# A fused recurrent attention and feed-forward kernel: half of unit 0's r and k in the gate's memory, its stateless products first, and TensorE's early waits filled with zeros

## The chip, the cores and the metric

The kernel runs on one core of one Trainium2 chip. The metric is the device time of one execution in microseconds (us). One more execution is recorded by the hardware profiler; its span runs from the first to the last instruction.

## What is computed

For 4 batches, 8 heads, 768 tokens and heads of 48, a recurrence with a state of 48 x 48 per head runs over the tokens, and its output goes through a feed-forward layer from 384 to 2048 and back, all in float32:

```
for t in range(S):
    kt, vt, rt, wt = (k[:, :, t], v[:, :, t], r[:, :, t], w[:, :, t])
    cur = np.einsum('bhd,bhe->bhde', u[None] * kt, vt)
    y[:, :, t] = np.einsum('bhd,bhde->bhe', rt, state + cur)
    state = wt[:, :, :, None] * state + np.einsum('bhd,bhe->bhde', kt, vt)
x = y.transpose(0, 2, 1, 3).reshape(B * S, H * D)
h = x @ w_in
g = np.where(h >= 1, h, np.where(h <= -1, 0.0, (h + 1) ** 2 / 4.0))
out = g @ w_out
```

## The kernel before, in words

**Units.** The 3072 tokens of all batches are cut into 12 units of 256 tokens; three units make a batch, and units 0, 3, 6 and 9 start from an empty state. In a unit the heads are split into two halves q of 128 rows, and the tokens into chunks of 64. `attention(u, ...)` lays out one unit:

- Loads on SyncE's queue: per half the scales w (`wq`, 128 x 521) and r and k together (`rk`, 128 x 1024); then v. For `wq` and `rk` there are three slots each, `slot = [(2u + 1 - q) % 3 ...]`: unit 0 takes slots 0 and 1, unit 1 takes 2 and 0. So unit 1's second load of r and k goes where unit 0's first half lies.
- VectorE scans: p, the running product of the scales (L473), and y, its inverse from the chunk's end (L468), one half after the other. Then k times y (L494) and r times p (L544), in place.
- For units 0 to 2, ScalarE makes k times u (L484), and TensorE multiplies it with r (`among`, L514, 32 small matmuls, which the trace records as 64). The result gives the diagonal, which VectorE picks into the tiles R (L520). A second `among` of k and r gives what lies below the diagonal, and two more picks. ScalarE copies the transposed k (L553, `ktrans`) to SBUF (L560).
- `umat` (L575) makes each chunk's k'v. The states follow one another: VectorE adds the old state to it (L593) and multiplies by p at the chunk's end (L594). For unit 0 (`CHAINED`) TensorE adds instead (L598), and VectorE only multiplies (L591).
- The output `y`: products with the earlier states in two orders (`cross`, `along`, L620), and products of R with v (also L620). The last are stateless: they need no state. Units 0 and 1 (`ALONE`) begin with banks cleared by TensorE (L655) and add to them, then spread the last heads' rows with a permutation (L703), and subtract their high part with a matmul (L694, the "subtracting triples"), so that ScalarE can copy a high and a low part to x (L684, L680).

**Steps.** The 12 units make 6 blocks of 512 tokens. A step is one block (or half block) and one of 16 slices f of the hidden layer: nine matmuls into a bank h (L989), the gate on ScalarE and VectorE (L790, L791, L792, L794, L795, into buffers g, gh, gl, three each), and nine matmuls into the output banks acc two to three steps later (L1009). Block 0 does its first 5 slices half by half, block 1 its first 14. The outputs of a block are copied to ob and to two of the g buffers and leave from there (L822, L823).

**Weights.** A slice's bits are loaded (L390), split by ScalarE (L402, L404), given their sign by GpSimd (L406; for f 9 by VectorE, `SIGNS`), joined by VectorE (L408), rounded by ScalarE to the high part (L398; VectorE for the slices in `SPLITS`), and the low part is left by VectorE (L411). `FLIGHT` is how many may be under way.

**Checks.** ScalarE checks every unit's scales (L746, L747). For the first `GUARDED` units that is done late, on a second load of the scales into the buffers fl; for the others in place.

**Order.** `Plan` collects all operations with costs, dependencies and due times (`SLACK`, `LEADS`, `DECODE` set them), simulates the engines and a load queue and keeps the best order of some tries. The engines then run their lists in that order; a list waits where its next instruction waits. `kept_warm` walks TensorE's list and, where the plan expects a wait, puts in matmuls of zeros (L360) into a bank that is to be begun afresh, up to a share `USE` of the last 3.4 us. At the very start 50 small matmuls of zeros are issued (L366).

Of the kernel before, what the change touches and what calls it, by code (L numbers as in the profile page):

```python
# [10 lines left out]
F32 = mybir.dt.float32  # L11
# [15 lines left out]
C = 64  # L27
# [17 lines left out]
USE, SPAN, COLUMN = 0.68, 3.4, 0.00168  # L45

COLD = 7.0

# [8 lines left out]
class Plan:  # L57
# [97 lines left out]
    def kept_warm(self, order, engine, banks, fill):  # L155

        ops, begin, end = self.ops, self.begin, self.end
        free, out, busy = 0.0, [], []
        used = {b: [n for n in order if b in ops[n]["touch"]] for b in banks}
        for n in order:  # L160
            op = ops[n]
            if op["e"] == engine:
                at = begin[n]
                use = sum(max(0.0, y - max(x, at - SPAN)) for x, y in busy)
                lack = min(USE * SPAN - use, at - free - 0.3)
                if free and lack > 0.15:
                    for b in banks:
                        after = next((m for m in used[b] if begin[m] >= at), None)
                        before = max((end[m] for m in used[b] if begin[m] < at), default=0.0)
                        if (after is None or ops[after]["fresh"]) and at - max(before, free) > lack:  # L170
                            out.append(lambda b=b, lack=lack, free=free: fill(b, lack, free))
                            busy.append((at - lack, at))
                            break
                free = at + op["cost"]
                busy.append((at, free))
            out.append(op["emit"])
        return out

    def order(self):
# [24 lines left out]
        while any(open_.values()):  # L204
# [18 lines left out]
            begin[n] = t  # L223
            free[e] = end[n] = t + op["cost"]
            if op["port"]:
                port = end[n]
                first.clear()
            if op["size"]:
                bus = max(bus, t) + op["size"] / 360e3
                end[n] = bus + 2.0  # L230
                lands.append(end[n])
# [24 lines left out]

SLACK = 2.03
LEADS = {0: 71.6, 1: 72.9, 2: 33.1, 3: 10.6, 4: 28.8, 5: 10.1, 6: 29.8, 7: 24.3, 8: 36.5, 9: 16.8, 10: 13.8, 11: -2.7}
LEAD, DECODE = 15, 12.7
FLIGHT = 3  # L260
FULL = 3

EARLY = 3

GUARDED = 6

APART = 1

# [3 lines left out]

SPLITS = set()
SIGNS = {9}
CHAINED = {0}
STEP, FIRST, PACED = 4.9, 24.0, 4.6
# [3 lines left out]
def attention_moe(tc, a):  # L280
# [41 lines left out]
    last = one([128, 2, UT], F32R, "last")  # L322
    g_ = tiles(LAG + 1, [128, WIDE], F32, "g")
    gh = tiles(LAG + 1, [128, WIDE], F32R, "gh")
# [29 lines left out]

    def zeros(to, n):

        while n >= 32:
            m = min(512, n if n < 128 else n // 128 * 128)
            rhs = zero[:, 0:m] if m <= 128 else zero.unsqueeze(1).broadcast_to([128, m // 128, 128])
            PE.matmul(to[:, 0:m], lhsT=zero, rhs=rhs, start=True, stop=True)  # L360
            n -= m
# [64 lines left out]
    def attention(u, when):  # L426
# [15 lines left out]

        slot = [(2 * u + 1 - q) % 3 for q in range(2)]
        pv = p_.rearrange("p (q n) c -> p q n c", q=2)

# [3 lines left out]
        for q in (1, 0):  # L449
            load(due, wq[slot[q]], a["w"][u, q], [("w", slot[q])])  # L450
            load(due, rk[slot[q]], a["rk"][u, q], [("k", slot[q]), ("r", slot[q])])
        if u == 0:
# [25 lines left out]
        def parts(q, i):  # L478
            return rk[slot[q]][:, i].rearrange("p (n c) -> p n c", c=C)

        def with_u(q):
            for pr in range(2):
                cs = slice(pr * UT, pr * UT + UT)
                A.mul(ku[:, q, cs], rk[slot[q]][:, 1, cs], u_col[:, 2 * q + pr : 2 * q + pr + 1])  # L484

        for q in (1, 0):
            s = slot[q]
            if early:
                op("ACT", 1.0, due, [("k", s), "cst"], [("ku", q), "nk"], lambda q=q: with_u(q))
# [4 lines left out]
            op("DVE", 0.69, due, ["y"], [("k", s)], lambda q=q: V.tensor_tensor(  # L494
                out=parts(q, 1), in0=parts(q, 1), in1=y_.rearrange("p (n c) -> p n c", c=C + 1)[:, :, 1:], op=ALU.mult), port=True)
# [8 lines left out]
        def among(to, left):  # L504

            for pair in range(4):
                q, pr = divmod(pair, 2)
                for c2 in range(2):
                    for g in range(2):
                        for h in range(2):  # L510
# [4 lines left out]
                                bank[to[h]][HP * g : HP * g + C, lo : lo + C], lhsT=left(q)[i, cs],  # L515
                                rhs=rk[slot[q]][i, 0, cs], start=True, stop=True,
                            )
# [5 lines left out]

        both = [("r", slot[0]), ("r", slot[1])]
        if early:
# [17 lines left out]
        for q in (1, 0):  # L543
            op("DVE", 0.69, due, [("p", q)], [("r", slot[q])], lambda q=q: V.tensor_tensor(  # L544
                out=parts(q, 0), in0=parts(q, 0), in1=pv[:, q, :, 0:C], op=ALU.mult), port=True)
# [3 lines left out]
        def ktrans(q, b):  # L549
            for pr in range(2):  # L550
                for c2 in range(2):
                    lo = (pr * 2 + c2) * 128
                    PE.transpose(out=bank[b][:, lo : lo + 128], in_=rk[slot[q]][:, 1, tokens(q, 1, pr, c2)], identity=ident)  # L553

        op("PE", 1.2, due, [("k", slot[0]), ("k", slot[1]), *both], [("b", ba[0]), ("b", ba[1])],
           lambda: among(ba, lambda q: rk[slot[q]][:, 1]))
        for q in (1, 0):
            b = take()
            op("PE", 0.4, due, [("k", slot[q]), "cst"], [("b", b)], lambda q=q, b=b: ktrans(q, b))
            op("ACT", 0.6, due, [("b", b)], [("kt", q)], lambda q=q, b=b: A.copy(  # L560
# [61 lines left out]
        def inter(g, h, pair, c2):  # L622
            s = before[2 * c2 + g]
            if s is None:
# [3 lines left out]
            put(g, pair, h, c2, lhsT=st[s][i, pair * D : pair * D + M],  # L628
                rhs=rk[slot[q]][i, 0, tokens(q, 0, pr, c2, g)])

# [11 lines left out]
        def along():  # L642
            crossed(0)
            for two in (0, 2):
                for c2 in range(2):
# [13 lines left out]
        if alone:  # L659
            op("PE", 0.5, due, ["zero"], [("b", by[0]), ("b", by[1])], cleared)  # L660
        op("PE", 0.6, due, ss + [vk, ("r", slot[0]), ("r", slot[1])], [("b", by[0]), ("b", by[1])], cross, fresh=not alone)

        for g in range(2):
            op("ACT", 0.2, due, [("b", by[g])], [("look", g)], lambda g=g: A.copy(look[0:1, g : g + 1], bank[by[g]][0:1, 0:1]))
        op("PE", 1.65, due, ss + [("R", 0), ("R", 1), vk, ("r", slot[0]), ("r", slot[1])],
           [("b", by[0]), ("b", by[1])], along, fresh=False)

# [201 lines left out]
    with tc.manual_schedule(engines=None):  # L869
        for emit in plan.kept_warm(plan.best(step_ops, dues), "PE", [("b", i) for i in range(8)],  # L870
                                   lambda b, us, at: zeros(bank[b[1]], int(us / COLUMN / (2 if at < COLD else 1)))):
            emit()
# [204 lines left out]
```

## Time and profile before

| | |
|---|---|
| median of 3 runs | 521.43 us (520.64 to 522.26) |
| profiled execution | 520.55 us, span 519.0 us |
| mean granted TensorE clock | 0.998 |
| TensorE busy | 504.5 us, 97% |
| VectorE busy | 340.9 us, 66% |
| ScalarE busy | 299.2 us, 58% |
| GpSimd busy | 86.8 us, 17% |
| first products of the first step (L989) | begin at 32.43 us |

In the rows below a time is counted from the start of the span. A row of the timeline has start, length, engine, line, operation, output and inputs, the number of instructions, and in brackets the idle time ahead and what ended it. A row of a group has its count, busy time, mean in ns, and the idle time before with its releasers. A row of the waits says who waited for whom, the total, how often, and the longest. Engine names are PE (TensorE), DVE (VectorE), ACT (ScalarE), POOL (GpSimd), SPq (SyncE's queue).

### The profile page before, as it was taken

How to read it: one execution, taken by the hardware profiler on the slowest of the kernel's cores; microseconds unless marked ns; L12 is line 12 of the kernel's file. 1: busy time of each engine (PE TensorE's matmuls, PEld its weight loads, DVE VectorE, ACT ScalarE, POOL GpSimd, SP SyncE). 2: the span in 40 equal slices, each digit the busy share in tenths (PEclk: the TensorE clock that was granted, in tenths of full speed). 3: DMA queues.
4: the chain of work that ended last, by engine and by line, in shares of the span. 5: the costliest groups of instructions: out<-in, count | busy, mean ns of one | idle time of the engine just before them, and what ended most of it. 6: DMA issues, size and time to landing. Idle time of an engine off the chain costs nothing.

```text
span 519.0 us, 13075 instructions
## 1 busy us (share of the span) xinstructions
PE 504.5 (97%) x5550; PEld 419.4 (81%) x5550; DVE 340.9 (66%) x597; ACT 299.2 (58%) x615; POOL 86.8 (17%) x60
## 2 busy tenths in 40 slices
PE   7989999999999999999999999999999999999995
PEld 5768988887899998877778878788888787788884
DVE  5999999979797979543979535895353445233332
ACT  3688888878865566543646544565444435444441
POOL 1654627511303030101020101110000100000000
PEclk9999999999999999999999999999999999999999
DMA  8794916147714152302262203230100100100001
GB/s 309 292 366 168 354 63 230 51 138 230 245 44 157 55 205 52 117 2 77 74 208 52 114 0 124 88 128 1 63 1 0 42 18 12 67 1 0 1 0 66
DMA packets 21762, 54.69 MB, mean 105 GB/s; under 512 B 3008, under 2 KB 8640, under 8 KB 21696
## 3 DMA queue, kind: packets, MB, share of 16 engines
q1 hardware_dynamic: 21552, 53.65, 29.8%
q8 instruction: 45, 0.74, 0.6%
q14 instruction: 21, 0.17, 0.1%
q10 hardware_dynamic: 144, 0.13, 0.1%
HBM read 47.09 MB, written 4.72 MB: 100 GB/s over the span
## 4 chain that ended last, share of the span: by engine, by line
PE 80%; DVE 5%; DMA 5%; ACT 4%; issue 2%; POOL 1%; SPq 0%; POOLq 0%; DVEq 0%; ACTq 0%
PE acc L1009 34%; PE h L989 34%; PE bank L620 4%; PE bank L514 2%; DMA rk<-in_rk 2%; PE bank L575 2%; PE bank L553 2%; DMA wraw<-in_wbits 1%; DVE r L520 1%; DMA out_y<-g 1%; DVE p L473 1%; DMA fl<-in_w 1%; POOL wraw L406 1%; DVE wt L411 1%; DVE fl L408 1%
## 5 line engine op out<-in xcount | busy, mean ns | idle before, releaser
L989 PE MATMUL h<-x,wt 128*128 128x512 f32 (+1 forms) x1035 | 223.3, 362 | 1.2 <-DVE g L792 1.2
L989 PEld LDWEIGHTS h<-x,wt 128*128 128x128 f32 x1035 | 171.1, 188 | 32.6 <-DVE g L792 1.9
L1009 PE MATMUL acc<-gh,wt 128*128 128x512 f32 (+1 forms) x690 | 157.1, 362 | 0.0
L792 DVE SCALAR_TENSOR_TENSOR g<-g,h 128x512 f32<-128x512 f32 (+1 forms) x115 | 68.0, 593 | 103.3 <-ACT g L791 98.8
L1009 PEld LDWEIGHTS acc<-gh,wt 128*128 128x128 f32 x690 | 115.6, 188 | 21.2
L790 ACT ACTIVATE g<-h 128x512 f32<-128x512 f32 (+1 forms) x115 | 60.4, 525 | 117.4 <-PE h L989 112.5
L795 DVE TENSOR_TENSOR gl<-g,gh 128x512 fp32r<-128x512 f32 (+1 forms) x115 | 73.7, 642 | 32.1 <-ACT gh L794 31.5
L794 ACT CAST gh<-g 128x512 fp32r<-128x512 f32 (+1 forms) x115 | 62.6, 546 | 44.2 <-DVE g L792 42.6
L1009 PE MATMUL acc<-gl,wt 128*128 128x512 f32 (+1 forms) x345 | 86.9, 358 | 0.0
L1009 PEld LDWEIGHTS acc<-gl,wt 128*128 128x128 f32 x345 | 59.6, 188 | 10.9 <-DVE gl L795 0.2
L791 ACT ACTIVATE g<-g 128x512 f32<-128x512 f32 (+1 forms) x115 | 64.6, 562 | 3.2
L406 POOL TENSOR_SCALAR wraw<-fl 128x768 uint16<-128x768 f32 x15 | 48.8, 3279 | 46.4 <-ACT wraw L404 42.3
L540 POOL TENSOR_TENSOR r<-cst,d 128x512 f32<-128x512 f32 x18 | 18.8, 1065 | 195.8 <-PE bank L620 178.7
L473 DVE TENSOR_TENSOR_SCAN p<-wq,seeds 128x520 f32<-128x520 f32 x24 | 31.3, 1304 | 3.0 <-DMA wq<-in_w 2.2
L532 POOL TENSOR_TENSOR nk<-nk 128x768 f32<-128x768 f32 x9 | 17.0, 1885 | 84.5 <-DMA nk<-in_nk 84.5
L468 DVE TENSOR_TENSOR_SCAN y<-wq,seeds 128x520 f32<-128x520 f32 x24 | 30.5, 1270 | 0.8
L494 DVE TENSOR_TENSOR rk<-rk,y 128x512 f32<-128x512 f32 x24 | 18.0, 751 | 1.2 <-ACT nk L484 0.8
L620 PEld LDWEIGHTS bank<-rk,st 64*64 64x64 f32 (+1 forms) x656 | 12.2, 133 | 7.2 <-issue 3.6
L593 DVE TENSOR_TENSOR sm<-bank,st 128x192 f32<-128x192 f32 x37 | 13.1, 355 | 6.7 <-PE bank L575 5.7
L404 ACT ACTIVATE wraw<-wraw 128x768 uint16<-128x768 uint32 x16 | 17.3, 1084 | 0.2
L560 ACT COPY kt<-bank 128x512 f32<-128x512 f32 x24 | 13.6, 587 | 6.5 <-PE bank L553 5.5
L553 PE MATMUL bank<-cst,rk 128*128 128x128 f32 x96 | 14.9, 287 | 2.5 <-DVE rk L494 2.0
(102 smaller groups left out, 399.9 us busy)
## 6 DMA issues: line engine op xcount, KB each, us to landing
rk<-in_rk SPq DMA_DIRECT2D x24, 512.0 KB, 5.4
wraw<-in_wbits SPq DMA_DIRECT2D x16, 768.0 KB, 7.9
nk<-in_nk SPq DMA_DIRECT2D x9, 768.0 KB, 4.5
wq<-in_w SPq DMA_DIRECT2D x24, 260.5 KB, 2.8
vn<-in_v SPq DMA_DIRECT2D x12, 384.0 KB, 6.3
fl<-in_w SPq DMA_DIRECT2D x12, 260.0 KB, 4.2
out_y<-g SPq DMA_DIRECT2D x11, 256.0 KB, 2.4
x<-last SPq DMA_DIRECT2D x60, 32.0 KB, 2.3
```

What stands on the lines that cost most here:

```text
L406: op(on, 0.62 if f in SIGNS else 3.2, due, [("fl", k)], [("raw", f)], lambda: e.tensor_scalar(out=half(1), in0=s, scalar1=0.0, scalar2=327 ...
L468: V.tensor_tensor_scan(out=y_[:, ::-1], data0=w[:, SEG:0:-1], data1=sv[:, ::-1], initial=0.0, op0=ALU.mult, op1=ALU.add)
L473: V.tensor_tensor_scan(out=pv[:, q].rearrange("p n c -> p (n c)"), data0=w[:, 0:SEG], data1=sv, initial=0.0, op0=ALU.mult, op1=ALU.add,)
L553: PE.transpose(out=bank[b][:, lo : lo + 128], in_=rk[slot[q]][:, 1, tokens(q, 1, pr, c2)], identity=ident)
L620: PE.matmul(out=bank[by[g]][HP * half : HP * half + M, lo : lo + C], start=first, stop=False, skip_group_check=True, **kw)
L790: op("ACT", c, due, [("b", 6 + hk)], [("g", gk)], lambda: nc.scalar.activation(gs, hs, AF.Relu, scale=0.5, bias=0.5))
L791: op("ACT", c, due, (), [("g", gk)], lambda: nc.scalar.activation(gs, gs, AF.Square))
L792: op("DVE", 0.13 + 0.53 * k, due, [("b", 6 + hk)], [("g", gk)], lambda: nc.vector.scalar_tensor_tensor(out=gs, in0=gs, scalar=1.0, in1=hs, ...
L794: op("ACT", c, due, [("g", gk)], [("gh", gk)], lambda: nc.scalar.copy(ghs, gs))
L795: op("DVE", 0.15 + 0.5 * k, due, [("g", gk), ("gh", gk)], [("gl", gk)], lambda: nc.vector.tensor_tensor(out=gls, in0=gs, in1=ghs.bitcast(F ...
L989: nc.tensor.matmul(hp, lhsT=wx[f][:, cs], rhs=xt[:, j, :], start=n == 0, stop=n == 8)
L1009: nc.tensor.matmul(o[j], lhsT=wx[f][:, cs], rhs=gt, start=first and i == 0, stop=stop and i == 2, skip_group_check=True)
```

## The change

1. Unit 0's half 1 takes its r and k not in an `rk` slot but in the first two of the three g buffers, which become parts of one tile (`gates`). Slot 0 is thus free for unit 1 from the start.
2. In units 0 and 1 the stateless products (`inner`) come first, then the products with the states (`along`, `cross`); each was one list before, with the stateless ones last.
3. `kept_warm` fills planned waits of TensorE up to 16 us of its plan wholly, and up to 0.3 us beyond; and it may now add zeros to a bank that is already begun (`held`, without `start`), if TensorE itself wrote to it before and after.
4. The plan counts TensorE's operations before 9 us twice, and loads at 300 KB/us up to 8 us, 390 after.
5. The table of numbers that sets the order is new. `FLIGHT` goes from 3 to 8, `GUARDED` from 6 to 3, the slices 1, 4, 5, 8, 9 are rounded on VectorE, the signs of 9, 10, 14, 15 are made on VectorE, and no unit is `CHAINED`.

```diff
-                lack = min(USE * SPAN - use, at - free - 0.3)
+                lack = at - free - 0.3 if at > EAGER else at - free + LATE if at - free > 0.15 else 0.0
+                if at > EAGER:
+                    lack = min(USE * SPAN - use, lack)
...
+                        held = after is not None and before is not None and not ops[after]["fresh"] and all(
+                            ops[m]["e"] == engine for m in (before, after)) and end[before] <= free
...
-FLIGHT = 3
+FLIGHT = 8
...
-GUARDED = 6
+GUARDED = 3
...
-SPLITS = set()
-SIGNS = {9}
-CHAINED = {0}
+SPLITS = {1, 4, 5, 8, 9}
+SIGNS = {9, 10, 14, 15}
+CHAINED = set()
...
+        rks = [rk[s] for s in slot]
+        rkey, kkey = ([(n, s) for s in slot] for n in "rk")
+        if u == 0:
+            rks[1], rkey[1], kkey[1] = gates[:, 0:2], ("g", 0), ("g", 1)
...
-            PE.matmul(to[:, 0:m], lhsT=zero, rhs=rhs, start=True, stop=True)
+            PE.matmul(to[:, 0:m], lhsT=zero, rhs=rhs, start=not add, stop=True, skip_group_check=add)
...
+        if alone:
+
+            op("PE", 1.1, due, [("R", 0), ("R", 1), vk], outs, inner, fresh=False)
+            op("PE", 0.55, due, ins, outs, along, fresh=False)
+            looks()
+            op("PE", 0.6, due, ins, outs, cross, fresh=False)
```

What this does to the order is seen at three places. The first is SyncE's queue at the start of the program; wq0 and wq1 are the scales of halves 1 and 0 of unit 0, rk0 and rk1 its r and k, wq2 and rk2 unit 1's first half. Before:

```order
L340 DMA wq0_78<-in_w 128x521
L340 DMA wq1_79<-in_w 128x521
L340 DMA cst0_67<-in_consts 128x196
L340 DMA rk0_81<-in_rk 128x1024
L340 DMA nk0_84<-in_perm 128x384
L340 DMA rk1_82<-in_rk 128x1024
L340 DMA vn0_85<-in_v 128x2x384
L390 DMA wraw0_197<-in_wbits 128x1536
```

And now, up to unit 1's two loads of r and k (rk2 and rk0):

```order
L349 DMA wq1_79<-in_w 128x521
L349 DMA nk0_84<-in_perm 128x384
L349 DMA cst0_67<-in_consts 128x196
L349 DMA wq0_78<-in_w 128x521
L349 DMA g0_103<-in_rk 128x1024
L349 DMA rk1_82<-in_rk 128x1024
...
L349 DMA wq2_80<-in_w 128x521
L349 DMA rk2_83<-in_rk 128x1024
L349 DMA rk0_81<-in_rk 128x1024
```

The scales of half 1 went from first to fourth, and unit 1's second r and k from twentieth to thirteenth. The second place is VectorE's list from unit 0's picks on; acc0, acc1 hold the products of k times u, acc2 and h0 those of k, st1 to st4 are the states, wq2 is unit 1's. Before:

```order
L520 COPY_PREDICATED r1_91<-cst0_67,acc1_117 128x512
L591 TENSOR_TENSOR st1_94<-h1_120,ptot0_76 128x192
L472 MEMSET seeds0_73 128x8
L473 SCALAR_TENSOR_TENSOR p0_87<-wq2_80,seeds0_73 128x520
L591 TENSOR_TENSOR st2_95<-bank2_123,ptot0_76 128x192
L520 COPY_PREDICATED r0_90<-below0_71,acc2_118 128x512
L520 COPY_PREDICATED r1_91<-below0_71,h0_119 128x512
L591 TENSOR_TENSOR st3_96<-h1_120,ptot0_76 128x192
L467 RECIPROCAL seeds0_73<-p0_87 128x8
L468 SCALAR_TENSOR_TENSOR y0_88<-wq2_80,seeds0_73 128x520
L591 TENSOR_TENSOR st4_97<-bank2_123,ptot0_76 128x192
```

And now:

```order
L534 COPY_PREDICATED r1_91<-below0_71,h0_117 128x512
L605 TENSOR_TENSOR st1_94<-h1_118,ptot0_76 128x192
L607 TENSOR_TENSOR sm0_99<-bank2_121,st1_94 128x192
L608 TENSOR_TENSOR st2_95<-sm0_99,ptot0_76 128x192
L607 TENSOR_TENSOR sm0_99<-h1_118,st2_95 128x192
L608 TENSOR_TENSOR st3_96<-sm0_99,ptot0_76 128x192
L607 TENSOR_TENSOR sm0_99<-bank2_121,st3_96 128x192
L608 TENSOR_TENSOR st4_97<-sm0_99,ptot0_76 128x192
L486 MEMSET seeds0_73 128x8
L487 SCALAR_TENSOR_TENSOR p0_87<-wq2_80,seeds0_73 128x520
```

Unit 1's first two scans went behind unit 0's states, and each state now takes two operations. The third place is TensorE's list from the first zeros to unit 0's first products of k (acc2) or `umat`; nk holds k times u, bank0 to bank2 the transposes or zeros, and g the memory of half 1. Before:

```order
L360 MATMUL bank_121<-zero_74 128x512
L360 MATMUL bank_121<-zero_74 128x128
L360 MATMUL bank_121<-zero_74 128x48
L553 MATMUL bank_121<-cst_67,rk_81 128x128 x4
L514 MATMUL acc_116<-rk_82,nk_84 64x64
...
L553 MATMUL bank_122<-cst_67,rk_82 128x128 x4
L360 MATMUL bank_121<-zero_74 128x128
L360 MATMUL bank_121<-zero_74 128x81
L575 MATMUL h_120<-vn_85,kt_92 64x48 x2
L575 MATMUL bank_123<-vn_85,kt_92 64x48 x2
```

And now:

```order
L369 MATMUL bank_119<-zero_74 128x512 x3
L369 MATMUL bank_119<-zero_74 128x128
L528 MATMUL acc_114<-rk_82,nk_84 64x64
...
L528 MATMUL acc_115<-g_103,nk_84 64x64
L567 MATMUL bank_119<-cst_67,g_103 128x128 x4
L369 MATMUL bank_120<-zero_74 128x512
L369 MATMUL bank_120<-zero_74 128x128
L567 MATMUL bank_120<-cst_67,rk_82 128x128 x4
L369 MATMUL bank_119<-zero_74 128x512
L369 MATMUL bank_119<-zero_74 128x128
L369 MATMUL bank_119<-zero_74 128x121
L528 MATMUL acc_116<-rk_82 64x64
```

Zeros of 1,664 columns (688 before) now stand ahead of the first products, the transposes of half 1 come behind these, 640 columns stand ahead of the transposes of half 0 and 761 ahead of the products of k, which come before `umat`. In the whole list the columns of zeros go from 4303 to 6217, and the one fill that stood at the seam between blocks 0 and 1 (256 columns) is gone.

More of the change, by code (lines that the diff above doesn't have):

```diff
@@ L45 @@
 USE, SPAN, COLUMN = 0.68, 3.4, 0.00168
+EAGER, LATE = 16.0, 0.3
+RISES = 9.0
 COLD = 7.0
@@ L223, in order @@
             begin[n] = t
-            free[e] = end[n] = t + op["cost"]
+            free[e] = end[n] = t + op["cost"] * (2 if e == "PE" and t < RISES else 1)
             if op["port"]:
@@ L322, in attention_moe @@
     last = one([128, 2, UT], F32R, "last")
-    g_ = tiles(LAG + 1, [128, WIDE], F32, "g")
+    gates = one([128, LAG + 1, WIDE], F32, "g")
+    g_ = [gates[:, i] for i in range(LAG + 1)]
     gh = tiles(LAG + 1, [128, WIDE], F32R, "gh")
@@ L522, in picked @@
                 data=bank[of].rearrange("p (n c) -> p n c", c=C))
-        both = [("r", slot[0]), ("r", slot[1])]
+        both = [*rkey]
         if early:
```

59 lines of the change are left out of this document (32 added, 27 removed).

## The prediction

> **What bounds the kernel now.** I read the busy time by stage first, since the share over the whole span (97% for TensorE) is an average. The columns are the stretch, its length, then busy time and instructions of TensorE, weight load, VectorE, ScalarE and GpSimd, then granted clock, DMA share and GB/s.
>
> ```profile
> 24.00:51.00 27.00, 24.85 (x451) 20.86 (x450) 25.70 (x43) 22.65 (x48) 14.53 (x5) 1.00 0.71 269
> 51.00:118.00 67.00, 67.00 (x705) 56.90 (x705) 61.58 (x97) 56.23 (x104) 31.19 (x12) 1.00 0.49 174
> 118.00:134.00 16.00, 14.16 (x249) 12.07 (x248) 13.96 (x28) 14.29 (x38) 3.57 (x3) 1.00 0.73 236
> 134.00:505.00 371.00, 370.97 (x3682) 307.76 (x3681) 219.29 (x401) 191.07 (x402) 27.50 (x21) 1.00 0.20 65
> ```
>
> From 134 us on TensorE never stops, and the change leaves its products there alone, so that stage can't move. From 51 to 118 us it doesn't stop either, but VectorE is busy 61.58 of 67 us, so it has 5.4 us to give. Time can be won or lost in two places: before 51 us, where VectorE is busy with hardly a hole, and at the seam between blocks 0 and 1 (118 to 134 us).
>
> Then the waits at the start. VectorE waits for its first scale load, for ScalarE's k times u, and twice for TensorE; after that it runs through:
>
> ```profile
> 3.82 1.24 DVE L473 TENSOR_TENSOR_SCAN p<-wq,seeds 128x520 f32<-128x520 f32 x1 [2.18 <-DMA wq<-in_w]
> 8.84 0.69 DVE L494 TENSOR_TENSOR rk<-rk,y 128x512 f32<-128x512 f32 x1 [0.85 <-ACT nk L484]
> 11.01 0.69 DVE L494 TENSOR_TENSOR rk<-rk,y 128x512 f32<-128x512 f32 x1
> 12.68 1.29 DVE L544 TENSOR_TENSOR rk<-rk,p 128x512 f32<-128x512 f32 x2 [0.98 <-PE acc L514]
> 16.04 0.36 DVE L591 TENSOR_TENSOR st<-h,ptot 128x192 f32<-128x192 f32 x1 [0.80 <-PE h L575]
> 21.25 0.33 DVE L591 TENSOR_TENSOR st<-bank,ptot 128x192 f32<-128x192 f32 x1
> 31.38 1.74 DVE L544 TENSOR_TENSOR rk<-rk,p 128x512 f32<-128x512 f32 x2
> ```
>
> On the loads, SyncE can issue unit 1's second r and k only at 23.20, when unit 0 has left the slot; ScalarE waits for it at 28.81.
>
> ```profile
> 23.20 0.33 SPq L340 DMA_DIRECT2D rk<-in_rk x1
> 6.58 0.31 ACT L455 ACTIVATE minus<-cst 128x128 fp32r<-128x128 f32 x1 [4.32 <-DMA cst<-in_consts]
> 7.90 0.91 ACT L484 ACTIVATE nk<-rk,cst 128x256 f32<-128x256 f32 x2 [0.92 <-DMA rk<-in_rk]
> 9.68 0.91 ACT L484 ACTIVATE nk<-rk,cst 128x256 f32<-128x256 f32 x2 [0.79 <-DMA rk<-in_rk]
> 28.81 0.91 ACT L484 ACTIVATE nk<-rk,cst 128x256 f32<-128x256 f32 x2 [0.27 <-DMA rk<-in_rk]
> ```
>
> **The change part by part.** When TensorE makes the second subtracting triple of unit 1 (L694), it has five first products of block 0 and two second products behind it, in both orders. Before makes it here, in the chain that ended last:
>
> ```profile
> 49.58 1.11 PE h L989 x9
> 50.68 0.28 PE bank L694 x3
> ```
>
> So the end of that triple, 50.96 us, is the mark; how much earlier the new kernel passes it is the first term.
>
> *The first scale load goes from first to fourth in SyncE's queue.* VectorE still begins with the scan of half 1, whose load now stands behind the other scale load, perm and the constants: 260.5 + 192 + 98 + 260.5 = 811 KB to its end, by the shapes in the order. Before, the first three loads (two scales and the constants, 619 KB) were in at 6.58 by ScalarE's wait, and with 512 KB of r and k at 7.90: 512 KB in 1.32 us. The 192 KB beyond 619 take 0.5 us, so the first scan starts at 7.1 instead of 3.82. Bounds: 5.5, were the wait at 6.58 the constants' own, and 7.9. I take the interpolation between the nearest rows.
>
> *What VectorE saves of that.* From its first scan to the end of the second k times y it took 11.70 - 3.82 = 7.88 us, of which 0.85 was a wait for k times u. That is made by 9.3 now, so 7.03 us: 14.1. TensorE's first products need only k times u, whose second half still comes from the sixth load (9.68 + 0.91), so they begin at 10.6 as before and are done long ahead; the 0.98 goes too. The two r times p (1.29) end at 15.4. TensorE's queue then holds the transposes of half 0 (they need 14.1) and 761 columns of zeros. The nearest row for zeros has 595 columns (512 + 83):
>
> ```profile
> 20.43 1.21 PE L360 MATMUL bank<-zero 128*128 128x512 f32 x4
> 54.15 1.16 PE L514 MATMUL bank<-rk,nk 64*64 64x64 f32 x64
> L593 DVE TENSOR_TENSOR sm<-bank,st 128x192 f32<-128x192 f32 x37 | 13.1, 355 | 6.7 <-PE bank L575 5.7
> L594 DVE TENSOR_TENSOR st<-sm,ptot 128x192 f32<-128x192 f32 x37 | 13.5, 366 | 1.3
> ```
>
> 761 columns take 1.5 us, so zeros hold the products of k up to 16.0, 0.6 us after their inputs. They take 1.1 (the second row, less its overlap), the u-matrix 1.1 more: 18.2. VectorE picks from 17.1 to 18.4, then makes the four states; the three additions that TensorE did are now its own. 0.36 and three pairs of 0.72 with a hand-over of 0.06 make 2.7: the last state at 21.1, against 21.58. But before had put unit 1's first scan and back scan (2.8) among these, and now they follow.
>
> *The freed slot.* Unit 1's r and k are the 12th and 13th loads, behind nothing that waits for unit 0's end, so their k times u is no longer waited for: ScalarE does it behind f 0's cast and f 2's copy, up to 26.9 (before 29.72). What is late next is VectorE, whose prices are these:
>
> ```profile
> L473 DVE TENSOR_TENSOR_SCAN p<-wq,seeds 128x520 f32<-128x520 f32 x24 | 31.3, 1304 | 3.0 <-DMA wq<-in_w 2.2
> L468 DVE TENSOR_TENSOR_SCAN y<-wq,seeds 128x520 f32<-128x520 f32 x24 | 30.5, 1270 | 0.8
> L408 DVE SCALAR_TENSOR_TENSOR fl<-fl,wraw 128x768 int32<-128x768 int32 x16 | 15.7, 980 | 1.2 <-POOL wraw L406 1.2
> L411 DVE TENSOR_TENSOR wt<-fl,wt 128x768 fp32r<-128x768 f32 x16 | 15.1, 946 | 0.1
> L520 DVE COPY_PREDICATED r<-below,bank 128x512 f32<-128x512 int32 x22 | 15.0, 731 | 1.7 <-PE bank L514 1.5
> L406 DVE TENSOR_SCALAR wraw<-fl 128x768 uint16<-128x768 f32 x1 | 0.6, 606 | 0.0
> ```
>
> Neighbours overlap by some 0.1 us, so I take 0.87 for a join (L408) or a low part (L411), 0.63 for a pick, 0.6 for a product with y or p, 1.34 for a scan with its memset and 1.48 for a back scan with its reciprocal. From 21.1: scan, join of f 0, back scan, low part, scan, k times y, back scan, pick, two r times p, k times y; that is 10.5 us, so unit 1's operands are whole at 31.6; before, the row at 31.38 ends at 33.1. Up to the low part of f 3 there follow three joins (2.6), f 1's cast (0.45, half of the low part's row; bounds 0.3 and 0.95), three picks (1.9), three low parts (2.6), four state pairs (3.1) and a gate (0.4): 11.0, which is 42.6. The fourth half step starts there. It (1.1), half of the state products (0.5), two second products (2.2), the spread (1.3), the fifth step (1.1) and two triples (0.6) make 6.8 to the mark: 49.4 against 50.96. **First term: -1.6 us**; bounds -3.2 (the load at 5.5) and +1.0 (zeros at the slow clock, below).
>
> *51 to 118 us.* VectorE gains five casts (0.45) and three sign steps (0.61), 4.1 us, beside an idle 5.4. Up to the low part of f 8 the new order leaves behind it three state pairs of unit 2 (2.3), a scan (1.3) and f 9's sign and join (1.5) that stood ahead of it, and adds four casts and the three state additions (2.9): 2.2 less, while it began 3.3 later less 2.6 us of waits. So I cost this at nothing; the cover is those 5.4 us, and without it TensorE waits for what is missing.
>
> *The seam.* Here before loses 1.2 + 0.6 us in waits and 0.5 in zeros:
>
> ```profile
> PE h L989 <- DVE g L792: 1.2, 2, 0.9
> PE bank L575 <- ACT kt L560: 0.6, 1, 0.6
> 129.24 0.59 PE L360 MATMUL bank<-zero 128*128 128x256 f32 x2
> 131.49 0.38 ACT L790 ACTIVATE g<-h 128x256 f32<-128x256 f32 x1 [1.14 <-DMA out_y<-g]
> L746 ACT ACTIVATE fl<-fl 128x520 f32<-128x520 f32 x12 | 7.6, 631 | 4.5 <-DMA fl<-in_w 4.5
> L747 ACT ACTIVATE fl<-fl,minus_one 128x520 f32<-128x520 f32 x12 | 8.7, 729 | 0.3
> ```
>
> Twelve late scale checks of 1.4 us lie on ScalarE around the seam; six stay, the others follow their own units, and no zeros stand there any more. But a gate buffer is still waited for until its output has left, the 1.14 above, and unit 3's products now come behind the first two steps of block 1. **Second term: -1.0**, bounds -2.3 (all of it) and +1.3 (one more such wait).
>
> The sum is -2.6. The profiled execution took 520.55 (span 519.0), so 517.95; the median of the runs shown is 0.88 above it, so 521.43 - 2.6 = 518.8.
>
> **The rivals.** *VectorE becomes the bound (slower).* If a cast costs what the low part does (0.95), the additions are 4.7 + 1.8 + 1.1 = 7.6 us against 5.4 idle; with unit 2's scan and back scan (2.8) moved behind the gates TensorE would wait 5.0 us from 51 to 118. For it: 92% busy there. Against it: the count above. 521.43 - 1.6 - 1.0 + 5.0 = 523.8; it decides once the extra work passes 5.4 us.
>
> *The zeros run at the slow clock (no change).*
>
> ```profile
> 1.86 2.98 PE L366 MATMUL h<-zero 64*64 64x32 f32 x100 [1.86 <-POOL zero L345]
> 4.77 2.79 PE L360 MATMUL bank<-zero 128*128 128x512 f32 x6
> 10.63 1.99 PE L514 MATMUL acc<-rk,nk 64*64 64x64 f32 x64
> ```
>
> The 64 records that took 1.16 us at 54.15 took 1.99 at 10.63, though TensorE had been busy from 1.86 to 7.56. If it stays slow up to 15.4, the 1,664 columns before the first products and the 640 after them take twice as long, and the products of k come 2.6 later: first term +1.0, total 521.4. For it: that row. Against it: nearly unbroken zeros from 4.8 on. [...]
>
> *Only the start gains.* The seam's waits move but stay: 521.43 - 1.6 = 519.8.
>
> *The scale load lands at 5.5.* VectorE's whole chain comes 1.6 earlier: 521.43 - 3.2 - 1.0 = 517.2, and 515.9 with the whole seam. That the slot isn't freed early, or the fill not made, the order rules out.
>
> **How the numbers follow.** About 0.3% (1.6 us) can be told from no change. Forecast 0.40 (518.8), only the start 0.20 (519.8), early load 0.15 (517.2), slow clock 0.11 (521.4), VectorE 0.14 (523.8). Faster by over 0.3%: 0.36 of the forecast, half of the second, all of the third, 0.61. Slower 0.14, the rest 0.25. The range, 516.0 to 522.6, leaves out the VectorE case and little else.
>
> **What would show it.** Right: VectorE's first scan at about 7, the last state of unit 0 near 21, ScalarE no longer waiting for unit 1's r and k, the mark near 49.4, and no TensorE waits from 51 to 118. Wrong: a scan before 6, the mark after 51, the first products at 10.6 taking 2 us, or TensorE waiting for a gate or a low part after 51.

## The result

The changed kernel is slower: 525.86 us in the median of 6 runs (523.32 to 527.6), against 520.37 of the kernel before beside it; the ratio is 1.0109, 95% interval 1.0086 to 1.0131. Forecast were 518.8 us and a gain. The profiled execution took 527.6 us, 7.05 more than that of before; it was the longest of the six, and between the medians the loss is 5.5.

Where it went is told by the mark, the end of unit 1's second subtracting triple (L721 now): 57.19 us (56.74 + 0.45) against 50.96, 6.2 later. From there to the end of the last second product it is 463.6 us against 462.65, 1.0 more. So nearly all is lost at the start. By stage (columns as in the prediction), first two stretches of before, then the changed kernel:

```profile
16.00:24.00 8.00, 6.75 (x191) 4.94 (x183) 7.86 (x13) 5.23 (x9) 7.71 (x3) 1.00 0.67 234
24.00:32.00 8.00, 7.01 (x94) 4.91 (x93) 7.58 (x11) 6.66 (x14) 2.16 (x2) 1.00 1.01 390
16.00:24.00 8.00, 4.65 (x192) 3.88 (x184) 6.97 (x15) 1.98 (x3) 6.04 (x2) 0.84 1.03 411
24.00:32.00 8.00, 8.00 (x72) 6.62 (x72) 3.51 (x6) 4.49 (x12) 0.00 (x0) 0.52 1.02 412
51.00:118.00 67.00, 66.90 (x693) 57.24 (x693) 65.16 (x103) 58.89 (x112) 25.91 (x8) 1.00 0.34 114
```

In the changed kernel TensorE is busy 4.65 of 8 us from 16 to 24 us, and from 24 to 32 it runs at half clock (0.52), while VectorE, which was to set the pace, is busy 3.51 of 8 (7.58 in before). The DMA engines are full in both stretches (share 1.03 and 1.02; in before 0.67 in the first). From 51 to 118 us TensorE hardly stops. TensorE's timeline shows what stood at 18 us, ScalarE's and VectorE's what came of it:

```profile
18.27 0.70 PE L634 MATMUL acc<-r,vn 64*48 64x64 f32 x29
22.32 1.30 PE L634 MATMUL acc<-r,vn 64*48 64x64 f32 x35 [3.35 <-issue]
25.85 0.20 ACT L682 COPY look<-acc 1x1 f32<-1x1 f32 x2 [7.84 <-PE acc L634]
28.16 0.83 ACT L407 CAST wt<-fl 128x768 fp32r<-128x768 f32 x1
29.03 0.96 DVE L420 TENSOR_TENSOR wt<-fl,wt 128x768 fp32r<-128x768 f32 x1 [4.44 <-ACT wt L407]
```

Unit 0's stateless products (64 records, two for each product) break off after the 29th, in the middle of a product, and go on 3.35 us later. "issue" means that the profile shows nothing that TensorE waited for. ScalarE's look (L682), a copy of one element of each output bank, waits 7.84 us for TensorE; f 0's cast stands behind it in ScalarE's queue, and VectorE waits 4.44 us for the cast. The granted clock of this trace has its entries at 7.71, 21.36, 31.60, 134.00 and 137.42 us, whole multiples of 3.41 us from each other, so it is read here in windows of that length (columns: window, length, TensorE's busy time and records, clock, DMA share, GB/s):

```profile
14.54:17.95 3.41, 3.41 (x135) 1.00 1.03 418
17.95:21.36 3.41, 1.02 (x31) 1.00 1.02 398
21.36:24.77 3.41, 2.45 (x41) 0.50 1.04 424
28.19:31.60 3.41, 3.41 (x17) 0.50 1.01 414
31.60:35.01 3.41, 2.63 (x71) 1.00 1.03 389
```

The stop leaves 1.02 us of work in the window up to 21.36, and the three windows after it run at half clock. At the seam one wait for an output that leaves from a gate buffer is left, longer than the 1.14 us of before; it too was followed by a window at half clock (134.0 to 137.4 us):

```profile
131.16 0.38 ACT L817 ACTIVATE g<-h 128x256 f32<-128x256 f32 x1 [2.48 <-DMA out_y<-g]
132.50 1.32 PE L1016 MATMUL h<-x,wt 128*128 128x256 f32 x9 [2.12 <-DVE g L819]
```

What does "issue" hide? The trace has a queue (q8) that brings instructions in packets of 16,384 bytes. I take it for TensorE's: its 45 packets are 0.74 MB, some 66 bytes for each of TensorE's 11,100 records, and the other engines together have only 1,999. One such packet began at 19.77 us and ended at 20.86, inside the stop, with the data queue full around it. Between 8.8 and 19.7 us the view of the DMA queues has no packet of this kind; from 19.7 to 21 us it has (packets, MB, share of 16 engines):

```profile
q1 hardware_dynamic: 166, 0.49, 97.2%
q8 instruction: 1, 0.02, 5.2%
```

Counted in the trace, TensorE had begun 698 weight loads and matmuls when it stopped (705 records with those of its sequencer). When the first packet of this kind begins (7.82 us) it is at 211 records, when the 44th does (517.46 us) at 11,130: 254 from packet to packet in the mean. Record 467, which the expectations name, begins at 16.3 us; that the packet is called for there is my estimate, which goes with these counts (211 and 254 make 465), and this trace doesn't show it. Whether TensorE stopped because the packet came late is what the experiments ask.

Theory T1: TensorE runs out of instructions, because a run of small products (128 records of products of k, 128 of the u-matrix, 128 stateless) is used up too soon (the last 255 of the 698 began within 2.57 us), while the packet stands behind data in full queues. T2: the packet takes that long whatever the queues hold, and only the dense run matters. T3: the stateless products wait for something that the profile doesn't show. S1: the wait at the seam is the gate buffers held by leaving outputs.

### The profile page after: what moved, and what is told of

It is laid out like the page before. It is cut to its first block, busy times and chain, and to the rows that moved or that the text cites. A ratio compares the mean times of both kernels' runs of the same rounds, so it can differ in the third digit from the quotient of the medians.

```text
span 526.0 us, 13099 instructions
## 1 busy us (share of the span) xinstructions
PE 509.3 (97%) x5550; PEld 422.6 (80%) x5550; DVE 346.7 (66%) x608; ACT 295.9 (56%) x610; POOL 79.2 (15%) x57
## 4 chain that ended last, share of the span: by engine, by line
PE 89%; DVE 6%; DMA 2%; issue 2%; ACT 1%; SPq 0%; DVEq 0%; ACTq 0%
PE acc L1036 38%; PE h L1016 37%; PE bank L634 4%; PE bank L589 2%; PE bank L528 2%; PE bank L567 2%; PE bank L369 1%; DMA out_y<-g 1%; DMA wq<-in_w 1%; DVE fl L417 1%; PE acc L634 1%; DVE y L482 1%; DVE rk L558 1%; DVE rk L508 1%; DVE r L534 1%
## 5 line engine op out<-in xcount | busy, mean ns | idle before, releaser
L822 DVE TENSOR_TENSOR gl<-g,gh 128x512 fp32r<-128x512 f32 (+1 forms) x115 | 71.6, 624 | 30.0 <-ACT gh L821 29.5
L415 POOL TENSOR_SCALAR wraw<-fl 128x768 uint16<-128x768 f32 x12 | 41.0, 3435 | 51.9 <-ACT wraw L413 50.4
L420 DVE TENSOR_TENSOR wt<-fl,wt 128x768 fp32r<-128x768 f32 x16 | 15.8, 989 | 4.5 <-ACT wt L407 4.4
L534 DVE COPY_PREDICATED r<-below,bank 128x512 f32<-128x512 int32 x22 | 15.5, 732 | 4.9 <-PE bank L528 4.3
L508 DVE TENSOR_TENSOR rk<-rk,y 128x512 f32<-128x512 f32 x23 | 17.4, 759 | 1.0 <-DMA rk<-in_rk 0.8
L413 ACT ACTIVATE wraw<-wraw 128x768 uint16<-128x768 uint32 x16 | 17.4, 1085 | 0.2
```

Of the source, the lines that this page charges most:

```text
L415: op(on, 0.62 if f in SIGNS else 3.2, due, [("fl", k)], [("raw", f)], lambda: e.tensor_scalar(out=half(1), in0=s, scalar1=0.0, scalar2=327 ...
L508: op("DVE", 0.69, due, ["y"], [kkey[q]], lambda q=q: V.tensor_tensor(out=parts(q, 1), in0=parts(q, 1), in1=y_.rearrange("p (n c) -> p n c" ...
L822: op("DVE", 0.15 + 0.5 * k, due, [("g", gk), ("gh", gk)], [("gl", gk)], lambda: nc.vector.tensor_tensor(out=gls, in0=gs, in1=ghs.bitcast(F ...
```

## The experiments

The kernel before took 520.1 to 520.6 us in the median beside each group of runs.

**Stateless products later.**

```diff
+        inner = next(e for e in emits if e.__name__ == "inner")
+        at = emits.index(inner)
+        emits[at : at + 1] = [lambda: zeros(bank[0], 512, False)] * 4
+        emits.insert(1 + next(i for i, e in enumerate(emits) if e.__name__ == "along"), inner)
```

> The changed kernel, but unit 0's 32 stateless products stand behind the first half of its products with the states, as before the change, with four 512-column zeros in their old place; all loads as in the changed kernel. T1 and T2 (a dense run of 384 small records outruns the next packet): TensorE has some 5 us for 256 records, so the packet is late by 1.2 us at most, the clock stays up, the mark is at 50 to 52 us, and the time is 518.5 to 521.5. T3 (a wait that belongs to a stateless product): the stop of 3 us goes with them to their new place, and the time stays at 524 or more.

520.24 us, ratio 1.0005 (0.9977 to 1.0033; a run of 1721 us is not in it). No stop, no half clock, mark at 52.25 us:

```profile
22.61 1.08 PE L634 MATMUL acc<-r,vn 64*48 64x64 f32 x60
51.81 0.45 PE L721 MATMUL bank<-x,minus 128*128 128x128 f32 x3
```

By T3 the stop would have gone with the products; it didn't. The mark is a little later than T1's 50 to 52 us, since the look of ScalarE, and f 0's cast behind it, now wait for the products in their new place (VectorE: 1.48 us for the cast).

**Fewer records ahead.**

```diff
-WARM = 50
+WARM = 30
...
+        zeros(hp[0], 512, False)
```

> The changed kernel with 20 of its 50 first warming products replaced by one 512-column product of zeros: 76 records fewer ahead of the same work. T1 and T2 (an instruction boundary): the stop moves 76 records on, out of the stateless products, which run through in 0.9 us, to the zeros and the first products with the states behind them, where TensorE starts again at 22.5 to 23.5 us; part of it then lies beside the states (ready at 21.1), the clock falls all the same, and the time is 523 to 526.5. T3 (a wait of its own): the stop stays inside the stateless products, behind the 29th record.

```profile
18.12 1.11 PE L635 MATMUL acc<-r,vn 64*48 64x64 f32 x64
19.79 0.25 PE L635 MATMUL acc<-rk,st 64*48 64x64 f32 x1
22.56 0.27 PE L635 MATMUL acc<-rk,st 64*48 64x64 f32 x4 [2.52 <-issue]
18.14:21.55 3.41, 1.90 (x68) 1.00 1.03 402
```

With 76 records fewer (half of them matmuls) the stop came 38 matmuls later: the other 35 records of the stateless products, 2 of zeros, and one of a product with a state. TensorE stopped again when it had begun 698 weight loads and matmuls. The place goes with the count of instructions and not with the product that stands there, and T3 has fallen. The time is 523.18 us (ratio 1.005, 1.0022 to 1.0078). Wrong was that the clock must fall: in the profiled execution the stop was parted by two windows, of which the first kept 1.90 us of work; the clock stayed at 1.0 and the mark was at 51.97 us. That execution took 518.99 us at a granted clock of 0.999; the nine others took 520.9 to 525.1, and the five above 523 had 0.991 to 0.993.

**The old rule for the zeros.**

```diff
-EAGER, LATE = 16.0, 0.3
+EAGER, LATE = 0.0, 0.3
```

> The changed kernel with the old rule for the zeros at the start (what the rule on the last 3.4 us asks for, not the whole wait): 5 products of zeros fewer ahead of unit 0's products of k, the rest as in the changed kernel. Z1 (the early full clock makes the dense run outrun its instructions): the clock opens only at 14 to 16 us, the run of small products takes up to 1 us more, the stop shrinks to 2.5 us or less, and the time is 521 to 525. Z2 (the zeros matter to neither): the stop stays at 3 us or more, and the time is 524 to 527.

```profile
18.36 0.82 PE L634 MATMUL acc<-r,vn 64*48 64x64 f32 x39
22.36 0.89 PE L634 MATMUL acc<-r,vn 64*48 64x64 f32 x24 [3.18 <-issue]
```

525.16 us, ratio 1.011 (1.0071 to 1.0149): Z2. Five products of zeros, 20 records, are missing, and the stop stands 10 matmuls later, again at 698 weight loads and matmuls. The early zeros neither make the loss nor mend it.

**A quiet queue, three attempts.** The first gate was badly chosen: the weight loads of f 2 to 7 stand behind a one-element transfer that reads unit 0's first picked matrix.

```diff
+    def wait():
+        nc.sync.dma_start(out=x_[1][0:1, 0, 0, 0:1].bitcast(F32), in_=r_[0][0:1, 0, 0, 0:1])
...
+        emits = [e for e in emits[:at + 1] if e not in late] + [wait] + late + emits[at + 1:]
```

> [...] Theory T1 (TensorE stops for 3.35 us inside unit 0's stateless products because its instruction packet stands behind data in the full queues): the packet starts within 1.5 us of record 467 instead of 3.5, the stop is 1.3 us or less, the clock stays at 1.0 behind it, the second subtracting triple of unit 1 ends at 50 to 52 us instead of 57.19, and the time is 518.5 to 521. Theory T2 (the packet takes that long whatever the queues hold; only the dense run of small products matters): the stop stays at 3 us or more, and the time at 525 to 527. Theory T3 (a wait of that product that the profile doesn't show): stop and time stay as well.

521.17 us, ratio 1.0037 (1.001 to 1.0065), but this tells nothing of T1 and T2: the one-element transfer itself stood in the full queues (DMA share 1.03 from 16 to 24 us), and VectorE's next pick into that matrix had to wait for it:

```profile
18.98 0.73 DVE L534 COPY_PREDICATED r<-below,acc 128x512 f32<-128x512 int32 x1 [2.59 <-DMA x<-r]
```

The second gate reads the first state, and unit 1's r, k and v stand behind it too.

```diff
+        nc.sync.dma_start(out=x_[1][0:1, 0, 0, 0:1].bitcast(F32), in_=st[1][0:1, 0:1])
```

> The changed kernel, but SyncE issues unit 1's r, k and v and the weight loads from f 2 on only behind a one-element transfer that reads unit 0's first state (written at about 18.3 us, and not rewritten before unit 1). What is issued ahead is 4.4 MB, drained by about 14 us at the 390 GB/s of this stretch, so the queues are empty when TensorE crosses record 467 at 16.2 us. T1 (the instruction packet is late because it stands behind data): the packet starts before 17.5 us instead of 19.77, the stop inside the stateless products is 0.7 us or less, the clock stays at 1.0, the mark (end of unit 1's second subtracting triple) is at 50.0 to 51.2 us instead of 57.19, and the time is 517.5 to 519.8. T2 (a packet takes that long whatever the queues hold): the stop stays at 2.5 us or more, and the time is 521 to 527.

```profile
q8 instruction: 1, 0.02, 10.1%
16.00:18.00 2.00, 2.00 (x113) 1.57 (x102) 1.29 (x3) 1.73 (x2) 2.00 (x1) 1.00 0.04 8
18.05 0.70 PE L642 MATMUL acc<-r,vn 64*48 64x64 f32 x29
19.25 0.76 PE L642 MATMUL acc<-r,vn 64*48 64x64 f32 x35 [0.50 <-issue]
28.49 0.89 ACT L419 ACTIVATE fl<-wraw 128x768 f32<-128x768 f32 x1 [4.64 <-DMA wraw<-in_wbits]
```

The first line is all that the DMA queues moved from 16.2 to 17.0 us. With the DMA share at 0.04 the packet began at 16.45 us, and the stop shrank to 0.50, behind the same 29th matmul. T1 holds, T2 has fallen. The time did not follow (524.67 us, ratio 1.01, 1.0062 to 1.0137): the loads came too late. f 2 was in at 28.49, ScalarE's k times u of unit 1 stands behind its copy, TensorE waited 4.7 us for that, the clock fell from 31.3 to 38.1 us, and the mark was at 56.12.

The third gate keeps unit 1's r and k early and reads r times p, which is done 3 us sooner.

```diff
+        nc.sync.dma_start(out=x_[1][0:1, 0, 0, 0:1].bitcast(F32), in_=gates[0:1, 0, 0:1])
```

> The changed kernel, but SyncE issues the weight loads from f 2 on and unit 1's v only behind a one-element transfer that reads unit 0's r times p (written at about 15.1 us); unit 1's r and k stay early, so what made ScalarE wait in the second quiet-queue experiment (f 2 in at 28.5 us) is in by 22 us. 5.4 MB stand ahead, drained at about 16.4 us, where TensorE asks for its packet. T1 with nothing new late: the packet starts by 17.3 us, the stop inside the stateless products is 1 us or less, no half clock before the end, no wait of VectorE over 0.7 us between 18 and 36 us, the mark at 50.0 to 51.0 us, and the time 516.5 to 519, below the kernel before by 0.3 to 0.8%. Rival R1 (the start is bound elsewhere and the stop hid it): no stop, full clock, but the mark at 52 us as in the run with the stateless products later, and the time at 519.5 to 521.

In the profiled execution all of it came: packet at 16.71 us, stop 1.1, no half clock, mark 50.68, time 518.7; but the queues weren't empty yet (data at 88% from 16.7 to 17.6 us), and the packet took 1.75 us. Yet the 12 runs reach from 517.97 to 525.27 us (median 521.64, ratio 1.0031, 1.0002 to 1.006). The likely cause is a race: this gate doesn't wait for the products of k, so where these are late the loads can be ahead of the packet. The kernel with this gate and own buffers, below, shows such an execution.

**Own output buffers.**

```diff
-            o, ok = (ob, "ob") if j == 0 else (g_[j], ("g", j)) if cs.start == 0 else (fl[0], ("fl", 0))
+            o, ok = (ob, "ob") if j == 0 else (fl[j][:, 0:WIDE], ("g", j)) if cs.start == 0 else (fl[0], ("fl", 0))
```

> The changed kernel, but outputs 1 and 2 of block 0 leave from two buffers of the weights' conversion, idle by then, instead of the gate's buffers. Theory S1 (the 2.12 us wait at 130 to 132 us, and the half clock from 134.0 to 137.4, come from the gate's buffers being held by the leaving outputs): wait and half clock go, 132 to 138 us loses 2.0 to 3.8 us, and the time is 522 to 524. Theory S2 (something else is late there): a wait of about 2 us stays on another name, and the time is 525 to 527.

522.74 us (ratio 1.0041, 1.0009 to 1.0073), in S1's range. The stop at the start is still there (2.93 us), but behind the mark TensorE has no idle time over 0.25 us, and from the mark to the last product it takes 459.76 us instead of 463.6.

**Both, first with the second gate**, then with the scale load of half 1 in SyncE's first place again (`emits.insert(0, scale)`), then with the early gate.

> The kernel of the second quiet-queue experiment, and outputs 1 and 2 of block 0 leave from two idle buffers of the weights' conversion. S1 (the waits at the seam come from the gate's buffers being held by leaving outputs; without them the run with its own output buffers had no idle time of TensorE over 0.25 us behind the mark): another 0.8 to 1.6 us go, the time is 516 to 518.5, below both kernels. S2: no wait goes, the time is that of the second quiet-queue experiment within 0.5 us.

522.74 us (ratio 1.0057, 1.0025 to 1.0089): the wait for a leaving output went, but f 2 is as late as in the kernel without own buffers (28.75 us), so the time missed its range.

> The kernel with the quiet queue and its own output buffers, and the scale load of half 1 back in first place of SyncE's queue. Q1 (the first scan's start at 6.85 us instead of 3.82 costs the start): VectorE scans from 3.8 to 4.2 us, unit 0's products of k begin 0.8 to 2.5 us earlier, the mark moves by as much, and the time is 514.5 to 517. Q2 (k times u and the r and k loads set the products' start anyway): VectorE waits instead for ScalarE, the mark moves by less than 0.5 us, and the time is that of the kernel with the quiet queue and own buffers.

523.02 us (ratio 1.0064, 1.0041 to 1.0087). VectorE scanned from 3.78 us, but the mark moved by nothing (55.76 against 55.67). Of the 3.4 us that the scan came earlier, 2.5 are left at the end of r times p. There zeros that are sized for the later scan hold up the products of k, and VectorE waits for these:

```profile
3.78 1.24 DVE L495 TENSOR_TENSOR_SCAN p<-wq,seeds 128x520 f32<-128x520 f32 x1 [2.14 <-DMA wq<-in_w]
13.84 1.46 PE L377 MATMUL bank<-zero 128*128 128x512 f32 x6
16.45 0.77 DVE L542 COPY_PREDICATED r<-below,acc 128x512 f32<-128x512 int32 x1 [2.33 <-PE h L536]
```

Unit 0's last state still came 0.78 us earlier (20.59 against 21.37), but then f 2's load, which the gate holds back, was in at 28.59 us against 28.75, and TensorE waited 5.2 us for the k times u behind it (4.5 without the early scan). So Q2 has the size right and not the cause, and this run can't tell what the early scan is worth: neither fewer zeros nor the early scan without a late f 2 was tried.

> The same with outputs 1 and 2 of block 0 leaving from idle buffers of the weights' conversion. S1 (their wait at the seam is real work lost): no idle time of TensorE over 0.25 us between the mark and the end, another 0.6 to 1.5 us less, the time 515.5 to 518, below both kernels. S2 (the seam has slack elsewhere): as the kernel without it within 0.5 us.

Median of 12 runs 521.8 us, 516.82 to 525.44 (ratio of the nine shortest 0.9989, 0.9955 to 1.0022), inconclusive as to the sum: it has the early gate's race. In the profiled execution the clock was at half from 11.91 to 15.32 us and the products of k began at 17.96 (15.48 with the early gate alone), while f 2's load was issued at 15.93 (15.59): the packet began at 22.27, and TensorE stopped for 3.24 us, again behind the 29th matmul. The 12 runs fall into two groups: six of 516.8 to 520.1 us with a granted clock of 0.997 to 1.0, and six of 523.5 to 525.4 with 0.985 to 0.992. The seam kept its promise (no wait, 459.76 us behind the mark).

**A gate that can't lose the race.** It reads the first state, and only f 2 and later and unit 1's v stand behind it.

```diff
+        at = max(i for i, e in enumerate(emits) if getattr(e, "unit", None) == (0, 0))
+        late = [e for e in loads if e.__name__ == "fetch"][2:]
+        late[1:1] = [e for e in loads if getattr(e, "key", ("",))[0] == ("v", 1)]
```

> As the kernel with the early gate (SyncE holds back the weight loads from f 2 on and unit 1's v, unit 1's r and k stay early), but the gate reads unit 0's first state (about 18.3 us), which can only be there when the products of k and the packet's request are past. T1 (packet behind data or not decides): in every run the packet finds drained queues, the stop is 1.1 us or less, the mark at 50.0 to 51.0 us, no half clock between 8 us and the end, the runs lie within 3 us of each other instead of 7, and the median is 517 to 519.5. Rival R2 (the scatter of the early-gate runs is the clock's windows, which fall on other waits too): the runs scatter over 5 us or more as before and the median stays at 520.5 to 522.5.

> The same with outputs 1 and 2 of block 0 leaving from idle buffers of the weights' conversion. T1 and S1 (both the late packet and the held gate buffers cost): no idle time of TensorE over 0.25 us from the mark to the end, 1.0 to 1.6 us less than without, median 515.5 to 518, below the kernel before by over 0.4%. S2 (the seam's wait is covered): as without within 0.5 us.

Without own buffers 518.86 us (518.44 to 520.56, ratio 0.9983, 0.9966 to 1.0000), with them 517.63 us (517.31 to 518.56, ratio 0.9963, 0.995 to 0.9976), which is below both kernels. Both medians lie in T1's ranges, and the runs are 2.1 and 1.3 us apart where the early gate's were 7. Two details fell short: the first one's stop is 1.16 us where 1.1 was the limit, and the second one's gain on before is 0.37% where over 0.4 was expected. The first one's interval reaches up to no change. The first one's rows (DMA queues from 17.4 to 18.6 us, then TensorE and VectorE):

```profile
q8 instruction: 1, 0.02, 5.6%
q1 hardware_dynamic: 13, 0.02, 5.0%
18.19 0.70 PE L642 MATMUL acc<-r,vn 64*48 64x64 f32 x29
20.05 0.76 PE L642 MATMUL acc<-r,vn 64*48 64x64 f32 x35 [1.16 <-issue]
25.11 1.69 ACT L506 ACTIVATE nk<-rk,cst 128x256 f32<-128x256 f32 x4
42.18 0.95 DVE L428 TENSOR_TENSOR wt<-fl,wt 128x768 fp32r<-128x768 f32 x1
50.32 0.45 PE L729 MATMUL bank<-x,minus 128*128 128x128 f32 x3
```

The packet has the queues to itself, and the mark is at 50.77 us.

## Why the prediction was wrong

**VectorE's start: right.** First scan at 6.85 us (7.1 forecast), second k times y done at 13.77 (14.1), r times p at 14.98 (15.4), the last pick at 18.28 (18.4), the last state at 21.05 (21.1).

**The zeros: right, and the rival with the slow clock fell.** The first entry of the granted clock, at full, stands at 7.71 us (15.47 before), and the 64 records of the first products ran from 10.70 to 12.03 us, 1.33 us against 1.99. The run with the old rule, whose first entry stands at 15.17 us, lost as much; what the zeros are worth where TensorE doesn't stop wasn't tried.

**The first term from 18.2 us on: the step that failed.** Behind the u-matrix (18.2 us) the prediction adds up VectorE's times alone: "then makes the four states", and "From 21.1: scan, join of f 0, back scan, low part". What TensorE does meanwhile got no term. So it was taken that TensorE goes through the stateless products at their duration, and that ScalarE, which waits for TensorE before f 0's cast, has the cast ready for that low part. Instead TensorE stopped for its instructions (3.35 us) and went on at half clock, and the low part of f 0 began at 29.03 us after a wait of 4.44; with the gate on the state it began at 24.43. The order put 384 small records in a row without a gap, and the loads that the freed slot and the longer list of loads in flight brought forward filled the queues (DMA share 1.03 and 1.02 from 16 to 32 us); which of the two would do alone wasn't tried. Neither the dense run nor the full queues made the long stop alone: with the stateless products later (DMA share 1.03 from 16 to 24 us) TensorE didn't stop there, and with drained queues (0.04) it stopped for 0.50 us. Before had 256 such records and then pauses; its packet too began late (18.38 us, DMA share 1.02 up to 18.3), but TensorE then waited for the states anyway. The price: the mark is 7.8 us behind its forecast of 49.4. With the gate on the state it is 1.4 behind, so some 6.4 belong to the late packet. By the profiled execution with fewer records ahead (stop of 2.5 us, full clock, mark 51.97), some 5 of these are the half clock, and little is the stop itself. That split rests on one trace; the granted clocks of the runs, with fewer records ahead and with the early gate and own buffers, go the same way.

**The freed slot: right, once the stop is gone.** k times u of unit 1 was to be done by 26.9 us; it was at 31.39, and at 26.80 with the gate on the state.

**From there to the mark: 1.4 us mis-sized.** With the gate, the low part of f 3 is done at 43.13 instead of 42.6 (f 1's cast took 1.06 us, taken 0.45, bound 0.95), and from there to the mark it is 7.6 instead of 6.8 us.

**51 to 118 us: right.** VectorE is busy 65.16 of 67 us, more than before, but TensorE 66.90 (64.30 and 67.00 with the gate on the state). The rival in which VectorE is the bound fell.

**The seam, -1.0: right in size where the clock stays up.** From the mark to the end it is 460.99 us with the gate against 462.65 before, 1.7 less. In the changed kernel's profile the wait of 2.12 us was followed by a window at half clock, which by that clock costs about half of its 3.41 us (an estimate); so the term stood at +1.0, inside its bound of +1.3. The other 1.2 us lay in the gate's buffers, as the run with gate and own buffers shows (459.82).

The kernel with the gate takes 518.86 us, where 518.8 was forecast. That this fits to 0.1 us is luck: the forecast starts from the 521.43 us of the runs shown, and the kernel before took 520.1 beside the gate. Forecast was a gain of 2.6; the gate's is 1.2 between the medians, and 2.0 between the profiled executions, of which the mark has 0.2 and the stretch behind it 1.7. No rival of the forecast had a price for instructions, so none reached 525.86; the nearest, VectorE as the bound, would have given 523.8 for a cause that didn't come.

## What to carry to other kernels

Where small products follow each other without a pause, as the 384 records here, count their instructions, and look in the trace whether the DMA queues are full (here a share of 1.03) when a packet of instructions comes in; a stop named "issue" that moves when instructions ahead of it are taken away, as here by 38 matmuls for 76 records, goes with their count. Bringing loads forward wasn't free here, though nobody waited for the queue: loads that can wait were gated on the first state, behind the packet, and the stop fell from 3.35 to 1.16 us. A short stop of TensorE has to be priced with the clock windows after it: here 3.35 us without work were followed by three windows of 3.41 us at half clock.

## What the runs showed of the hardware

- Packets of 16,384 bytes, which I take for TensorE's instructions, took 0.88 to 1.42 us from start to end in the changed kernel's trace and 0.88 to 1.85 in that of before; the one at the stop took 1.09 us in the changed kernel, and 1.75 with the early gate. With full queues (DMA share 1.03) it began at 19.77 us, with drained ones (0.04) at 16.45. In eleven of the thirteen kernels made from the changed one, itself among them, TensorE stopped behind 698 weight loads and matmuls, whatever stood there, for 0.2 to 3.35 us; in each of them it went on 1.2 to 1.5 us after the packet's end (20.86 to 22.32 in the changed kernel). In the other two, with the first gate and with the stateless products later, it came to that place without a stop 1.5 and 1.8 us after the packet's end.
- The entries of the granted clock stand at multiples of 3.41 us from each other (7.71, 21.36 and 31.60 us in the changed kernel). Before the last products it fell after windows at full clock that had 0.67 (second gate), 0.83 (own output buffers), 1.02 (the changed kernel's start), 1.17 (own buffers with the early gate) and 1.50 us of TensorE's work (the changed kernel's seam); it stayed after windows with 1.48 (second gate), 1.90 (fewer records ahead), 1.92 (gate on the state) and 1.99 (the changed kernel, 7.71 to 11.12 us). In the changed kernel it stayed at half for three windows at the start and for one at the seam. The 2.12 us wait at the seam was followed by half clock, while 2.52 us parted by two windows (fewer records ahead) weren't. Where the windows lie differs from one execution to the next: one ends at 21.36 us in the changed kernel, at 21.55 with fewer records ahead and at 22.93 with own output buffers.
- One element that SyncE moved as a gate took its place behind the data in the full queues (first gate, DMA share 1.03): VectorE waited 2.59 us for it.
